# A fused attention and gated-unit kernel: the first batch's q loaded by GpSimd's casting DMA and transposed in bf16, k in five loads with the tail unit first, one DMA for the feature weights, and new order tables

## The chip, the cores and the metric

The kernel runs on one core of one Trainium2 chip. Its time is the device time in microseconds (us) of one execution; the runs of the kernel before took 214.36, 215.17 and 215.64 us, with a median of 215.17 us. The profile is of one further execution, whose time was 216.05 us; the span from its first to its last instruction is 214.3 us, so that 1.75 us lie around the span. A difference of about 0.5%, or 1.1 us, is the least that a measurement of this kernel can tell from no change.

## The reference

Eight batches of eight heads, 576 rows (`seq`) and 64 columns (`head_dim`). A linear attention with exponential features of both signs is followed by a gated unit with a causal filter of five taps:

```python
def phi(x):
    proj = np.einsum('bhsd,df->bhsf', x, w_phi)            # 64 -> 128 features
    proj = proj - np.max(np.abs(proj), axis=-1, keepdims=True)
    return np.concatenate([np.exp(proj), np.exp(-proj)], axis=-1)
q_p, k_p = (phi(q), phi(k))
kv = np.einsum('bhsf,bhsd->bhfd', k_p, v)
z = np.sum(k_p, axis=2)
num = np.einsum('bhsf,bhfd->bhsd', q_p, kv)
den = np.einsum('bhsf,bhf->bhs', q_p, z)[..., None] + 1e-06
x = num / den                                              # heads side by side: 512 columns
gate = 1.0 / (1.0 + np.exp(-gate_pre))                     # gate_pre: five taps of conv_w over x
out = gate * (x @ w_val) @ w_out
```

## The kernel before

**Tiling.** One batch holds 8 x 576 rows of q and as many of k. They are seen as 18 blocks of 128 columns, each block with two rows of 64 side by side, and the blocks are grouped into five units: `UNITS` has four units of four blocks and a tail unit of two (blocks 16 and 17). A batch passes through these stages: load of q, k and v; transposition of q and k (`qT`, `kT`); projection by the feature weights `W2` on TensorE (`kp` and `qm`, line 599); the maximum of the absolute value on VectorE (`kmax`, `qmax`, line 607); the exponentials on ScalarE (`kexp`, line 617, into the tile `KTIL`; `qexp`, line 732, into `QTIL`); the scaling of v on GpSimd (line 633); the products with the scaled v (line 643) and with q (line 744); the division (line 765); the gate (806), the value product (838) and the output product (860).

**What sets the order.** Nothing is scheduled when the kernel is built: the string `ORDER` gives the order in which the tasks of `build` are written out, `FLEX` gives the engine of each task that may run on several (A for ScalarE, D for VectorE, P for GpSimd), `BANKS` the PSUM banks, and `WARM` says ahead of which place in the order TensorE multiplies a tile of ones to no purpose (lines 514 and 517). Each engine takes its instructions strictly in that order, so an instruction that waits holds up all that stand behind it on its engine. The setup in `Emit.__init__` (constants, memsets, the weight load `c_w`) stands ahead of all tasks.

**The first batch.** Its k and q are loaded in fp32 by SyncE's queue into memory that the second batch's `KTIL` buffer needs later (`XN32`). k comes in four loads of 128x576, q in five, one to a unit, and after them comes the first batch's v (`loadv`, line 553). TensorE transposes each block in fp32 (`tp32`, line 558), and ScalarE or VectorE copies a unit out of PSUM with a cast to bf16 (`tc32`, lines 564 and 566). Two DMAs on ScalarE's queue load the same 64 rows of the feature weights into the two halves of `W32`; GpSimd casts them to `W2` (line 471), which every projection needs. A one-column copy named `hold` (line 531) makes GpSimd wait for q's last unit to land; behind it GpSimd's queue issues the casting loads of the second and third batch's q and k (line 572), of `w_val` (line 475) and of the second batch's v. The second batch is transposed in bf16 by TensorE (`tp16`, line 577) and copied out eight blocks at a time (`tc16`, line 582); from the third batch on DMA transposes do it (line 587). The loads by SyncE and ScalarE stand in the profile under "hardware_dynamic" queues (q1 and q10), those by GpSimd under "software_dynamic" (q0).

Of the kernel before, what the change touches and what calls it, by code (L numbers as in the profile page):

```python
# [16 lines left out]
B, H, S, D = 8, 8, 576, 64  # L17
# [7 lines left out]
NU = len(UNITS)  # L25
PEB = 1
# [10 lines left out]
    "16:7:1 16:7:1 16:7:0 16:7:0 16:7:0 16:7:0 16:7:0 16:7:0 16:7:0 16:7:0 16:7:0 16:7:0 16:7:0 16:7:0 16:7:0 16:7:0 "  # L37
    "16:7:0 16:7:0 "
# [43 lines left out]
)  # L82
FLEX = (
    "ADAADAAAAAPPDPPAPPPPPDDDDDDADDDDDDDPPDPPDPPPPPADDAAAAAPPDPPAPPPDPDDDDADDPPAPPAPPDPPDDDAADAAPPAPPAPPPPDDDAAAADPPAPPAPPP"
    "PDDDDADAAAPPDPPAPPPPPAADAAPDAPPDPPPPDADDDAA"
)
BANKS = (
    "0100170421234567014545456723670145320167456745014570123666230167676723676744233373266236723010101676701456767454545230"
    "1236767245013230123674545232301320532345450101670145452301674523014545016767001235446701456745672367246723670167454523"
    "0145672301012301452301452330167212672301234523452354235670123676767674545016723234501674501230146723444016745230145450"  # L90
    "1332401452301456767014567236745674501010123453672324423014545672345674253367010101010101452323672345676745670167010101"
    "45230145452367674554642323014523456767456723454501456701230145674522234545674567672355644"
# [21 lines left out]
def dve(n, ov=0.075):  # L114
    return n / 960.0 + ov
# [50 lines left out]
def build(plan, em=None):  # L166
# [16 lines left out]
    for b in range(B):  # L183

        if b == 0:
            last = A("lk", 0, 9, "SP", 0.3, None, rank=-1100)
            for w in "kq":
                lds = []
                for u in range(4 if w == "k" else NU):
                    pr = -1000.0 + (0 if w == "k" else 10) + u  # L190
                    last = A("l" + w, b, u, "SP", 0.65, fn("load32", w, u), [], rank=pr, lat=0.1)
                    lds.append(A("l" + w, b, u, "DMA", 0.9 if w == "k" else 0.2 * UNITS[u][1], None, [last], rank=pr))
                if w == "q":
                    hold = [None, A("lk", b, 0, "POOL", 0.15, fn("hold", HOLDU), [lds[HOLDU]], rank=-600)]
                for u, (c0, n) in enumerate(UNITS):
                    need = [lds[u]] if w == "q" else sorted(set(lds[J // 9] for J in (2 * c0, 2 * (c0 + n) - 1)), key=lambda t: t.idx)
                    pr = -900 + (0 if w == "k" else 50) + u
                    g = plan.group("tp", 1)
                    tp = A("kp", b, u, "PE", 0.22 * n, fn("tp32", w, u), need, g, 0, rank=pr)
                    h["x" + w, b, u] = A("kmax", b, u, ("DVE", "ACT"), (dve(n * P), act(n * P)), fn("tc32", w, u), [tp], g, rank=pr)  # L200
                    h["tp", w, u] = tp

        if b:
# [43 lines left out]
            for c in GB:  # L247
                if b == B - 1:
                    for x in h["gacc", c]:
                        x.deps += [x for x in (G("xk", b, 0), G("xq", b, 0)) if x is not None]  # L250
        if b == 1:
            g = plan.group("mqt", 1)
            cc = A("mqt", 0, 0, "PE", 0.5, fn("c_cw"), [G("tp", "q", 1)], g, rank=-500)
            cc = A("mqt", 0, 0, "DVE", 0.2, fn("c_cw2"), [cc], g, rank=-500)
            cgs = []
            for i in range(2):
# [689 lines left out]
```

## Time and profile before

| what | value |
|---|---|
| median of three runs | 215.17 us |
| time of the profiled execution | 216.05 us |
| its span | 214.3 us |
| busy: PE, ScalarE (ACT), VectorE (DVE), GpSimd (POOL) | 90%, 85%, 81%, 61% of the span |
| moved by DMA | 39.84 MB, 186 GB/s over the span |

A share of busy time over the whole span says little here, because the stages have other limits: at the start the engines wait for the first loads, in the middle three engines are nearly full at once, and at the end the last outputs are written. Rows of the timeline give the start in us, the length, the engine, the line, the operation and the tiles (written <- read); a name with a q behind the engine (SPq, ACTq) is an issue on that engine's queue. PEld is TensorE's loading of weights, which runs beside its products.

### The profile page before, as it was taken

What the parts mean: (1) busy time and instruction counts of PE and PEld (TensorE: products, weight loads), DVE (VectorE), ACT (ScalarE), POOL (GpSimd) and SP (SyncE); (2) the same over time, 40 slices, a digit from 0 to 9 for tenths busy, and PEclk for the clock granted to TensorE, in tenths of its full rate; (3) what the DMA queues carried; (4) which work ended last, traced back from release to release, by engine and by line L of the source; (5) the groups of instructions that cost most, each with busy time, mean ns of one, the idle gap of its engine ahead of it and who ended that gap; (6) DMA issues with size and microseconds to landing.
All of it is one profiled execution on the core that took longest, in us unless ns stands there. A gap on an engine that the chain in (4) does not pass through costs nothing.

```text
span 214.3 us, 8735 instructions
## 1 busy us (share of the span) xinstructions
PE 192.9 (90%) x3806; PEld 136.1 (64%) x3806; DVE 173.1 (81%) x258; ACT 181.1 (85%) x256; POOL 131.2 (61%) x167
## 2 busy tenths in 40 slices
PE   7995767898999999998999899999999999999990
PEld 6663455666665675766775667567776765888630
DVE  2679999989989988999988899989789978643630
ACT  3599999999999998999899998999999999544130
POOL 3577999992996199728990499459922578101100
PEclk9999999999999999999999999999999999999997
DMA  6999999569869968996999998999942606189095
GB/s 187 347 266 212 215 270 176 217 110 191 169 122 216 263 119 165 260 215 120 184 260 227 189 160 212 277 239 210 171 146 47 225 8 101 31 146 315 9 268 173
DMA packets 49425, 39.84 MB, mean 186 GB/s; under 512 B 33637, under 2 KB 39013, under 8 KB 49386
## 3 DMA queue, kind: packets, MB, share of 16 engines
q1 hardware_dynamic: 43088, 28.58, 56.6%
q0 software_dynamic: 6032, 10.49, 25.9%
q8 instruction: 30, 0.49, 0.9%
q10 hardware_dynamic: 266, 0.21, 0.3%
q14 instruction: 9, 0.07, 0.1%
HBM read 30.48 MB, written 9.44 MB: 186 GB/s over the span
## 4 chain that ended last, share of the span: by engine, by line
PE 48%; DVE 19%; ACT 17%; issue 7%; POOL 3%; DMA 2%; ACTq 0%; DVEq 0%; POOLq 0%
PE PS L860 10%; PE PS L838 10%; ACT KTIL L617 7%; PE PS L806 7%; DVE MQP L607 6%; ACT QTIL L732 5%; DVE MK L607 5%; PE PS L599 5%; PE PS L744 4%; PE PS L643 3%; DVE GV L844 2%; PE PS L719 2%; DMA W<-in_w_phi_dram 2%; DVE XN L765 2%; PE PS L864 2%
## 5 line engine op out<-in xcount | busy, mean ns | idle before, releaser
L617 ACT ACTIVATE KTIL<-PS 128x1024 bf16<-128x1024 f32 (+1 forms) x80 | 71.6, 966 | 3.0 <-PE PS L599 2.1
L633 POOL TENSOR_TENSOR VT<-VN,EK 128x1152 bf16<-128x1152 f32 x31 | 65.8, 2123 | 2.6 <-ACT EK L626 2.2
L732 ACT ACTIVATE QTIL<-PS 128x1024 bf16<-128x1024 f32 x64 | 61.7, 1049 | 1.9 <-PE PS L724 1.8
L705 POOL TENSOR_TENSOR RX<-MQR,ident 128x512 bf16<-128x512 bf16 (+1 forms) x35 | 34.3, 1008 | 36.6 <-DVE MQR L693 34.8
L607 DVE TENSOR_REDUCE MQP<-PS 128x8 bf16<-128x1024 f32 (+1 forms) x40 | 43.2, 1112 | 4.7 <-PE PS L599 3.2
L607 DVE TENSOR_REDUCE MK<-PS 128x8 f32<-128x1024 f32 (+1 forms) x40 | 44.1, 1112 | 3.5 <-ACT KTIL L617 2.3
L838 PE MATMUL PS<-XT,WV 128*128 128x288 bf16 x256 | 35.0, 286 | 0.3
L860 PE MATMUL PS<-WOUT,GV 128*128 128x512 bf16 x128 | 30.9, 379 | 0.1
L844 DVE SCALAR_TENSOR_TENSOR GV<-TH,PS 128x576 bf16<-128x576 bf16 x32 | 23.8, 749 | 7.7 <-PE PS L838 6.1
L838 PEld LDWEIGHTS <-WV 128*128 128x128 bf16 x256 | 23.8, 98 | 8.2 <-issue 1.9
L810 ACT ACTIVATE TH<-PS 128x576 bf16<-128x576 f32 x32 | 20.2, 675 | 5.6 <-DVE GV L844 3.1
L806 PE MATMUL PS<-XT,GW 64*64 64x288 bf16 x640 | 23.5, 285 | 0.4 <-DVE MK L607 0.2
L643 PE MATMUL PS<-VT,KTIL 64*128 64x65 bf16 x1152 | 22.6, 191 | 1.4 <-issue 0.6
L765 DVE TENSOR_TENSOR XN<-PS,RCP 128x512 bf16<-128x512 f32 x32 | 22.1, 692 | 1.1
L643 PEld LDWEIGHTS <-KTIL 64*128 64x128 bf16 x1152 | 20.7, 95 | 3.5 <-issue 2.1
L744 PEld LDWEIGHTS <-QTIL 128*128 128x128 bf16 x512 | 17.9, 97 | 7.1 <-issue 5.7
L657 ACT ACTIVATE OUTS<-PS 128x512 f32<-128x512 f32 x23 | 14.0, 617 | 9.9 <-PE PS L860 8.1
L744 PE MATMUL PS<-KV,QTIL 128*128 128x65 bf16 x512 | 19.7, 193 | 2.0 <-DVE KV L651 0.9
L806 PEld LDWEIGHTS <-GW 64*64 64x64 bf16 x640 | 18.0, 106 | 3.6 <-issue 1.9
L860 PEld LDWEIGHTS <-GV 128*128 128x128 bf16 x128 | 11.4, 98 | 12.7 <-issue 1.5
L599 PE MATMUL PS<-W,kT 64*128 64x128 bf16 x288 | 14.7, 221 | 3.3 <-ACT qT L566 1.3
L719 PE MATMUL PS<-qT,W 64*128 64x512 bf16 (+1 forms) x80 | 14.6, 361 | 3.0 <-DVE MQP L607 1.7
(80 smaller groups left out, 226.8 us busy)
## 6 DMA issues: line engine op xcount, KB each, us to landing
out_dram<-OUTS SPq DMA_DIRECT2D x32, 256.0 KB, 3.8
VN<-in_v_dram SPq DMA_DIRECT2D x7, 1152.0 KB, 6.2
KQN<-in_q_dram POOLq DMA_DIRECT2D x6, 576.0 KB, 6.6
KQN<-in_k_dram POOLq DMA_DIRECT2D x6, 576.0 KB, 10.0
KTIL<-in_k_dram SPq DMA_DIRECT2D x4, 288.0 KB, 3.8
VN<-in_v_dram POOLq DMA_DIRECT2D x1, 1152.0 KB, 19.0
KTIL<-in_q_dram SPq DMA_DIRECT2D x4, 256.0 KB, 4.5
out_dram<-OUTS SPq DMA_DIRECT2D x14, 64.0 KB, 2.6
```

Source lines behind the costliest of these rows:

```text
L607: self.nc.vector.tensor_reduce(o, self.two(t.grp, n * P).rearrange("p a (c f) -> p a c f", f=F), AX.X, ALU.max, apply_absolute_value=True)
L617: self.nc.scalar.activation(self.KTIL[b % 2][:, s, c0:c0 + n, :, :].rearrange("p c a f -> p a c f"), self.two(t.grp, n * P).rearrange("p a ...
L633: x.tensor_tensor(self.VT[g][:, s, :, 0:D], self.VN[b % 2][:, NC * g:NC * g + NC, :], e.to_broadcast([P, NC, D]), ALU.mult)
L643: nc.tensor.matmul(self.PS[:, t.grp.banks[ab], (s * 2 + x) * E1:(s * 2 + x + 1) * E1], self.KTIL[b % 2][rows, s, J // 2, J % 2, :], self.V ...
L705: self.nc.gpsimd.tensor_tensor(o, *wide(self.MQR[self.mq(b, u)][:, :], self.ident2), ALU.mult)
L732: self.nc.scalar.activation(o, i, AF.Exp, scale=1.0 - 2.0 * s)
L744: nc.tensor.matmul(self.PS[:, t.grp.banks[h // 4], (h % 4) * E1:(h % 4 + 1) * E1], Q[:, s, c % 2, h, (c // 2) * P:(c // 2 + 1) * P], self. ...
L765: nc.vector.tensor_tensor(o.rearrange("p (g h) d -> p g h d", g=ng), n[:, :, :, 0:D], rc.unsqueeze(3).to_broadcast([P, ng, 4, D]), ALU.mult)
L806: self.nc.tensor.matmul(self.PS[o * D:(o + 1) * D, t.grp.banks[par], 0:R], self.GW[r, jj, 4 - m, :], X[r, 4 * a + jj, :, HALO - 8 * s:HALO ...
L838: self.nc.tensor.matmul(self.PS[:, t.grp.banks[par], 0:R], self.WV[:, i, (2 * j + par) * D:(2 * j + par + 2) * D], X[:, 4 * par + i, :, HA ...
L844: nc.vector.scalar_tensor_tensor(out=self.GV[b % 3][:, j, :, :], in0=self.TH[j][:, :, :], scalar=1.0, in1=self.two(t.grp, R), op0=ALU.add, ...
L860: nc.tensor.matmul(self.PS[:, t.grp.banks[0], :], GV[:, j, c % 2, (c // 2) * XH:(c // 2) * XH + P], self.WOUT[:, j, c % 2, :], start=(j == ...
```

## The change

The first batch's q is no longer loaded in fp32 by SyncE. GpSimd issues two casting DMAs (`loadq0`) of blocks 8 to 17 and of blocks 0 to 7 into bf16, in that order, and TensorE transposes q in bf16 with `tp16`; ScalarE or VectorE copies out blocks 0 to 7, 8 to 15 and 16 to 17. `hold` now reads the last column of the load of blocks 8 to 17. k comes in five loads, the first of which (`KLOADS`) brings the columns of the tail unit alone (128x256) and the last the rest of that quarter (128x320). One DMA with a repeated source fills both halves of `W32`. The memset of `ONES` is cut in two, and all of the tables (`WARM`, `ORDER`, `FLEX`, `BANKS`) are new.

```diff
+KLOADS = [(3, 5, 9), (0, 0, 9), (1, 0, 9), (2, 0, 9), (3, 0, 5)]
...
-    "16:7:1 16:7:1 16:7:0 16:7:0 16:7:0 16:7:0 ...
+    "16:6:0 16:6:0 ... 16:6:1 16:6:1 16:0:2 18:1:3 71:6:2 203:3:1 80:6:2 76:1:2 "
...
-            for w in "kq":
-                lds = []
-                for u in range(4 if w == "k" else NU):
-                    last = A("l" + w, b, u, "SP", 0.65, fn("load32", w, u), [], rank=pr, lat=0.1)
+            for u in range(NU):
+                last = A("lk", b, u, "SP", 0.65, fn("load32", "k", u), [], rank=-1000.0 + u, lat=0.1)
...
+            for i in range(2):
+                last = A("lq", b, i, "POOL", 0.65, fn("loadq0", i), [], rank=-990.0 + i, lat=0.6)
+                lds.append(A("lq", b, i, "DMA", 2.2, None, [last], rank=-990.0 + i))
+            hold = [None, A("lk", b, 0, "POOL", 0.15, fn("hold"), [lds[1]], rank=-600)]
+            for i, (c0, n) in enumerate(((0, 8), (8, 8), (16, 2))):
+                tp = A("xq", b, i, "PE", 0.06 * n, fn("tp16", "q", b, c0, n), [lds[min(i, 1)]], g, 0, rank=-850 + i)
+                x = A("xq", b, i, ("DVE", "ACT"), (dve(n * P), act(n * P)), fn("tc16", "q", b, c0, n), [tp], g, rank=-850 + i)
...
-        nc.vector.memset(self.ONES[:, :], 1.0)
+        for c in ((0, P), (P, 512)):
+            nc.vector.memset(self.ONES[:, c[0]:c[1]], 1.0)
...
-        for i in range(2):
-            nc.scalar.dma_start(self.W32[i * D:(i + 1) * D, :], self.wphi[:, :])
+        nc.scalar.dma_start(self.W32[:, :], self.wphi[:, :].unsqueeze(0).to_broadcast([2, D, F]))
...
+    def loadq0(self, t, i):
+        sl = slice((0, 8)[i], (8, NC)[i])
+        self.nc.gpsimd.dma_start(self.N["q"][0][:, sl, :].rearrange("p y c -> p (y c)"), self.rows("q", 0)[:, sl.start * P:sl.stop * P])
```

The program's order shows the change at three places. The first is GpSimd's queue from the cast of the weights (`W`) to the loads of the second and third batch. Before:

```order
L458 MEMSET MQP_88 128x128
L471 CAST W_127<-W_126 128x128 [waits DMAHW2_49,DMAHW0_49]
L531 CAST HOLD<-KTIL_73 128x1 [waits DMAHW0_49]
L572 DMA QTIL_75<-in_q_dram 128x2304
L572 DMA QTIL_75<-in_k_dram 128x4x576
L572 DMA KQN_65<-in_q_dram 128x2304
L475 DMA WV<-in_moe_w_val_dram 128x4x512
```

and after the change:

```order
L468 MEMSET MQP_89 128x128
L480 CAST W_128<-W_127 128x128 [waits DMAHW0_49]
L543 DMA KTIL_73<-in_q_dram 128x1280
L543 DMA KTIL_73<-in_q_dram 128x1024
L539 COPY HOLD<-KTIL_73 128x1 [waits DMASW0_49]
L580 DMA QTIL_75<-in_q_dram 128x2304
L580 DMA QTIL_75<-in_k_dram 128x4x576
L484 DMA WV<-in_moe_w_val_dram 128x4x512
```

The first batch's two q loads (into the memory of `KTIL_73`) now stand behind the cast of the weights, and `hold` waits for the first of them. The second place is TensorE's queue in the first batch, after the weights' first use. Before, the second and third group of k's fp32 transposes (line 558) stand with projections (line 599) around them:

```order
L558 MATMUL PS<-ident_f,KTIL_73 128x128 [waits DMAHW3_49]
L558 MATMUL PS<-ident_f,KTIL_73 128x128 x3
L599 LDWEIGHTS kT_68 [waits Activation_49]
L599 MATMUL PS<-W_127,kT_68 128x128 [waits Pool_49]
...
L558 MATMUL PS<-ident_f,KTIL_73 128x128 [waits DMAHW5_49]
L558 MATMUL PS<-ident_f,KTIL_73 128x128 x3
L599 LDWEIGHTS kT_68 [waits DVE_49]
```

and after it, where line 566 is k's fp32 transpose, line 585 q's bf16 transpose and line 607 the projection:

```order
L566 MATMUL PS<-ident_f,KTIL_73 128x128 [waits DMAHW3_49]
L566 MATMUL PS<-ident_f,KTIL_73 128x128 x3
L585 LDWEIGHTS KTIL_73 [waits DMASW0_49]
L585 MATMUL PS<-ident,KTIL_73 128x128
...
L566 MATMUL PS<-ident_f,KTIL_73 128x128 [waits DMAHW4_49,Activation_49]
L566 MATMUL PS<-ident_f,KTIL_73 128x128 x3
L607 LDWEIGHTS kT_68
L607 MATMUL PS<-W_128,kT_68 128x128 [waits DVE_49]
```

Eight transposes of q, which wait for the first of GpSimd's loads (DMASW0), now stand between k's transposes of unit 0 and the first projection of that unit. The third place is the head of ScalarE's queue. Before:

```order
L472 DMA cw_141<-in_moe_conv_w_dram 5x512
L566 ACT_TABLE_LOAD
L566 CAST kT_68<-PS 128x512 [waits PE_49]
L617 ACTIVATE KTIL_72<-PS 128x2x4x128 [waits PE_49]
L566 CAST qT_70<-PS 128x512 [waits PE_49]
```

and after the change:

```order
L481 DMA cw_142<-in_moe_conv_w_dram 5x512
L625 ACT_TABLE_LOAD [waits DVE_49]
L625 ACTIVATE KTIL_72<-PS 128x2x2x128 [waits PE_49]
L625 ACTIVATE KTIL_72<-PS 128x2x2x128
L574 CAST kT_68<-PS 128x512 [waits PE_49]
```

The table load now stands behind a wait for VectorE's copy of the tail unit, and the tail unit's two exponentials come first. SyncE's queue holds the five k loads and then the first batch's v, none of which waits for anything. Over the whole program ScalarE gets 5 of the copies named `KV` where it had 10, 21 of the output copies where it had 23, and one large and one small copy of `XT` less; VectorE takes these over; the one scaling of v that VectorE did (and its small cast) goes to GpSimd.

More of the change, by code (lines that the diff above doesn't have):

```diff
@@ L36 @@
 WARM = (
-    "16:7:1 16:7:1 16:7:0 16:7:0 16:7:0 16:7:0 16:7:0 16:7:0 16:7:0 16:7:0 16:7:0 16:7:0 16:7:0 16:7:0 16:7:0 16:7:0 "
-    "16:7:0 16:7:0 "
+    "16:6:0 16:6:0 16:6:0 16:6:0 16:6:0 16:6:0 16:6:0 16:6:0 16:6:0 16:6:0 16:6:0 16:6:0 16:6:0 16:6:0 16:6:0 16:6:0 "
+    "16:6:1 16:6:1 16:0:2 18:1:3 71:6:2 203:3:1 80:6:2 76:1:2 "
 )
@@ L44 @@
 ORDER = (
[37 rows of a table removed]
[36 rows of a table added]
 )
 FLEX = (
-    "ADAADAAAAAPPDPPAPPPPPDDDDDDADDDDDDDPPDPPDPPPPPADDAAAAAPPDPPAPPPDPDDDDADDPPAPPAPPDPPDDDAADAAPPAPPAPPPPDDDAAAADPPAPPAPPP"
-    "PDDDDADAAAPPDPPAPPPPPAADAAPDAPPDPPPPDADDDAA"
+    "ADAADADAPPDPPDPPPPPDDDADDADDDDDDAPPDPPDPPPPPDDDAADAAPPDPPDPPDPPDDDDAAAPPAPPAPPPPPDDAAADADPPDPPAPPPPPDDDADADPPDPPAPPPPD"
+    "DDDADDDAPPAPPDPPPPPDADADPPDPPDPPDPPAADAAD"
 )
 BANKS = (
[L88 to L92, printed above, removed]
+    "2245023301674523012367012345236702014545672323452232344523012323450123674365363617345012301452323670167016745670101456"
+    "7674542301574670145670145014523207674567450123234523676701672301454523672346767522016767454567230161620123676701230101"
+    "6723230123234501454545230456743501232323232323673127367010123670167454545676745230101230101232672330767012367010123231"
+    "2046745674523452301454567234501674545450145545674260123456701230123225320101450145230167676723016767232345670101676734"
+    "676701450167454504516767454545670145236767670123454501670145016733234501010123452310550"
 )
@@ L186, in build @@
             last = A("lk", 0, 9, "SP", 0.3, None, rank=-1100)
-            for w in "kq":
-                lds = []
-                for u in range(4 if w == "k" else NU):
-                    pr = -1000.0 + (0 if w == "k" else 10) + u
-                    last = A("l" + w, b, u, "SP", 0.65, fn("load32", w, u), [], rank=pr, lat=0.1)
[L192 to L201, printed above, removed]
+            lds = []
@@ new lines, in build @@
+            for u in range(NU):
+                last = A("lk", b, u, "SP", 0.65, fn("load32", "k", u), [], rank=-1000.0 + u, lat=0.1)
+                lds.append(A("lk", b, u, "DMA", 0.9, None, [last], rank=-1000.0 + u))
+            for u, (c0, n) in enumerate(UNITS):
+                need = sorted(set(lds[i] for i, (hp, a, z) in enumerate(KLOADS) for J in (2 * c0, 2 * (c0 + n) - 1) if a <= J - 9 * hp < z), key=lambda t: t.idx)
+                g = plan.group("tp", 1)
+                tp = A("kp", b, u, "PE", 0.22 * n, fn("tp32", "k", u), need, g, 0, rank=-900 + u)
+                h["xk", b, u] = A("kmax", b, u, ("DVE", "ACT"), (dve(n * P), act(n * P)), fn("tc32", "k", u), [tp], g, rank=-900 + u)
+                h.setdefault(("tp0",), []).append(tp)
@@ new lines, in build @@
+            lds = []
+            for i in range(2):
[3 more added lines that the diff above has]
+            for i, (c0, n) in enumerate(((0, 8), (8, 8), (16, 2))):
+                g = plan.group("tp", 1)
+                tp = A("xq", b, i, "PE", 0.06 * n, fn("tp16", "q", b, c0, n), [lds[min(i, 1)]], g, 0, rank=-850 + i)
+                x = A("xq", b, i, ("DVE", "ACT"), (dve(n * P), act(n * P)), fn("tc16", "q", b, c0, n), [tp], g, rank=-850 + i)
+                h.setdefault(("tp0",), []).append(tp)
+                for u, (d0, m) in enumerate(UNITS):
+                    if c0 <= d0 < c0 + n:
+                        h["xq", b, u] = x
@@ L273, in build @@
                                        [kp] + [G("st", b - 2, i, x) for i in range(2) for x in range(2)]
-                                       + ([G("tp", w, i) for i in range(NU) for w in "kq"] if b == 1 else []), g)
+                                       + (G("tp0",) if b == 1 else []), g)
         eks = []
@@ L405, in __init__ @@
         spare = self.KTIL[1][:, :, :, :, :].rearrange("p s c a f -> p s (c a f)").bitcast(FP32)
-        self.XN32 = {w: spare[:, i, :] for i, w in enumerate("kq")}
+        self.XN32 = {"k": spare[:, 0, :]}
+        self.N["q"][0] = self.KTIL[1][:, 1, :, :, :].rearrange("p c a f -> p (c a f)")[:, 0:NR].rearrange("p (y c) -> p y c", c=2 * D)
         spare = self.QTIL[1][:, :, :, :, :].rearrange("p s a h r -> p (s a h r)")
@@ L527, in zero, with hold @@
                                       start=False, stop=True, skip_group_check=True)
-    def hold(self, t, u):
-        c = UNITS[u][0] * P
-        self.nc.gpsimd.tensor_copy(self.HOLD[:, :], self.XN32["q"][:, c:c + 1])
+    def hold(self, t):
+        self.nc.gpsimd.tensor_copy(self.HOLD[:, :], self.N["q"][0][:, NC - 1, 2 * D - 1:2 * D])
+    def loadq0(self, t, i):
+        sl = slice((0, 8)[i], (8, NC)[i])
+        self.nc.gpsimd.dma_start(self.N["q"][0][:, sl, :].rearrange("p y c -> p (y c)"), self.rows("q", 0)[:, sl.start * P:sl.stop * P])
     def holdx(self, t, b):
@@ L543, in load32 @@
         o = self.XN32[w]
-        if w == "q":
-            c0, n = UNITS[u]
-            sl = slice(c0 * P, (c0 + n) * P)
-            self.nc.sync.dma_start(o[:, sl], self.rows("q", 0)[:, sl])
-        else:
-            self.nc.sync.dma_start(o[:, u * 9 * D:(u + 1) * 9 * D], self.rows("k", 0)[:, u, :])
+        hp, a, z = KLOADS[u]
+        self.nc.sync.dma_start(o[:, (hp * 9 + a) * D:(hp * 9 + z) * D], self.rows("k", 0)[:, hp, a * D:z * D])
     def loadv(self, t, b):
```

2 lines of the change are left out of this document (1 added, 1 removed), and 73 rows, old and new, of the table ORDER.

## The prediction

> **What bounds the kernel now.** I read the slices of the page first, then a table of five stretches, then the timeline of the first 16 us.
>
> ```profile
> span 214.3 us, 8735 instructions
> PE   7995767898999999998999899999999999999990
> DVE  2679999989989988999988899989789978643630
> ACT  3599999999999998999899998999999999544130
> ```
>
> Each digit is the busy tenth of 5.4 us. After the first three or four slices ACT and DVE are full, and PE is full from about the ninth on; no engine bounds the whole.
>
> ```profile
> core 0: us, PE busy (x) PEld busy (x) DVE busy (x) ACT busy (x) POOL busy (x), PEclk, DMA share, GB/s
> 0.00:11.60 11.60, 9.76 (x68) 7.56 (x68) 4.94 (x10) 5.55 (x7) 5.82 (x19) 1.00 0.83 273
> 11.60:40.00 28.40, 20.34 (x442) 14.82 (x437) 26.98 (x40) 28.08 (x43) 25.38 (x25) 1.00 1.13 234
> 40.00:180.00 140.00, 134.61 (x2837) 94.19 (x2835) 125.82 (x184) 134.37 (x188) 97.06 (x119) 1.00 0.84 176
> 180.00:207.00 27.00, 26.61 (x462) 19.04 (x460) 14.63 (x25) 12.13 (x20) 2.96 (x7) 1.00 0.57 147
> ```
>
> From 11.6 to 40 us ACT works 28.08 of 28.4 us and DVE 26.98, while PE idles 8.06 us waiting for them. From 40 to 180 us PE and ACT have 5.4 and 5.6 us of idle time left, and in the next 27 us PE has 0.4. So a microsecond lost ahead of 11.6 us, where ACT works only 5.55 of 11.6 us, is carried to the end, but for what these few idle microseconds give back. The prediction is decided at the start.
>
> ```profile
> 0.74 1.22 ACTq L470 DMA_DIRECT2D W<-in_w_phi_dram  x2
> 2.77 1.28 ACT L566 ACT_TABLE_LOAD   x1 [2.77 <-issue]
> 5.76 0.29 POOL L471 CAST W<-W 128x128 bf16<-128x128 f32 x1 [3.21 <-DMA W<-in_w_phi_dram]
> 6.75 1.02 ACT L617 ACTIVATE KTIL<-PS 128x1024 bf16<-128x1024 f32 x1 [1.14 <-PE PS L599]
> 10.51 0.59 ACT L566 CAST qT<-PS 128x512 bf16<-128x512 f32 x1 [1.15 <-PE PS L558]
> 20.36 5.66 ACT L732 ACTIVATE QTIL<-PS 128x1024 bf16<-128x1024 f32 x6
> ```
>
> The weights' cast waits until 5.76 us for the second weight DMA, the first large exponential starts at 6.75, ACT is full from 10.51, and q's first exponential starts at 20.36. Six of those take 5.66 us, so one costs ACT 0.94 us in a row (they overlap a little).
>
> **The change part by part: when q lands.** This term decides. The new loads of q stand behind the weights' cast on POOL, and PE stands still at the first of q's transposes, since all of its other work is queued behind. What the trace says of GpSimd's loads:
>
> ```profile
> 43.42 0.59 POOL L572 DMA_DIRECT2D KQN<-in_q_dram  x1
> q0 software_dynamic: 10, 0.05, 112.6%
> ```
>
> The issue at 43.42 us met idle DMA engines, and its first packets show in the window from 44.5 to 45 (the row; the half microsecond ahead of it has none), so first packets come about 1.3 us after the issue began. With SyncE's queue busy it is otherwise:
>
> ```profile
> 8.13 0.73 POOL L572 DMA_DIRECT2D QTIL<-in_q_dram  x1
> q1 hardware_dynamic: 298, 0.68, 99.7%
> q0 software_dynamic: 13, 0.06, 30.0%
> q0 software_dynamic: 44, 0.20, 99.4%
> ...
> 68.98 0.61 POOL L572 DMA_DIRECT2D KQN<-in_q_dram  x1 [0.32 <-issue]
> q1 hardware_dynamic: 268, 0.61, 103.3%
> q0 software_dynamic: 18, 0.08, 97.6%
> ```
>
> Behind the issue at 8.13 stand the queues from 10 to 12 us (q1, SyncE's, alone), 12 to 13 and 13 to 14; behind that at 68.98 the windows 69.5 to 71 (q1 alone) and 71 to 71.5. Both times GpSimd's packets came only as SyncE's v load ran out, 4 and 2 us after the issue. Once they flow they bring 0.20 MB (of bf16) per us.
>
> ```profile
> KTIL<-in_k_dram SPq DMA_DIRECT2D x4, 288.0 KB, 3.8
> VN<-in_v_dram SPq DMA_DIRECT2D x7, 1152.0 KB, 6.2
> QTIL<-in_q_dram POOLq DMA_DIRECT2D x1, 576.0 KB, 8.5
> q1 hardware_dynamic: 274, 0.56, 79.6%
> q1 hardware_dynamic: 220, 0.37, 101.6%
> ```
>
> After the change SyncE's queue holds k (4 x 288 KB) and right behind it v (1152 KB), issued without a wait in six issues of some 0.44 us, so by 3.4 us; before, v was issued at 6.49 us, behind q. These are 2.36 MB. The queue brought 0.56 MB from 2 to 4 us and 0.37 MB from 7 to 8 (the last two rows). At 0.36 MB per us from 4 us on, k ends at (1.18 - 0.6) / 0.36 = 1.6, so 5.6 us, with the weights' packets 5.8, and v at 5.8 + 1.18 / 0.36 = 9.0 us.
>
> ```profile
> DMA to landing us min/median/max: 3.3/3.8/4.3
> ```
>
> Of the two weight DMAs (this row, and the issue at 0.74 above) one landed 3.3 and one 4.3 us after its issue. The single one should land between 4.0 and 5.0 us; I take 4.4. The cast starts 0.14 us behind the landing as before (5.62 to 5.76) and takes 0.29, so q is issued at 4.85 us and is ready to flow at 6.15: just after v has begun at 5.8. I take it that q waits for v, as in both cases above: packets from 9.0 us, 0.33 MB (128 x 1280 x 2 bytes) at 0.20 gives 10.65, and from the last packet to the landing 1.0 us, as for QTIL (0.59 MB from about 12.7 end at 15.65, landed at 8.13 + 8.5 = 16.63). **q's first load lands at 11.6 us**, the second at 12.9. The ends: 8.8 (q goes ahead of v: 6.15 + 1.65 + 1.0) and 12.5 (a weight DMA that is a microsecond slower, and slower first packets).
>
> [...]
>
> **What follows from the landing.**
>
> ```profile
> L558 PE MATMUL PS<-ident_f,KTIL 128*128 128x128 f32 x36 | 8.5, 391 | 0.1
> L577 PE MATMUL PS<-ident,QTIL 128*128 128x128 bf16 x36 | 2.7, 220 | 0.0
> 7.68 0.61 PE L599 MATMUL PS<-W,kT 64*128 64x128 bf16 x8
> 13.80 0.40 PE L599 MATMUL PS<-W,kT 64*128 64x128 bf16 x8
> ```
>
> After 11.6 us PE does eight bf16 transposes (8 x 2.7 / 36 = 0.6), four fp32 ones (4 x 8.5 / 36 = 0.95) and a unit's eight projections at the early rate (0.61), so unit 0's exponential starts at about 13.8 us. The rest of ACT's queue up to q's first exponential is eight large exponentials (8 x 0.94 = 7.5), a copy of 1024 columns (1.0), two of 256 (0.6), two casts of 512 (1.0) and two small exponentials (0.35): 10.45 us, so 24.3 us where before it was 20.36. Two more small exponentials follow it that came ahead of it before. **ACT is 4.2 us late there.** PE gives the same: before, its useful work by 11.6 us was 9.76 less 2.5 for the products of ones, so 7.3 us; after the change it has done 0.5 + 0.3 + 0.95, so 1.75, and saves 18 x (8.5 - 2.7) / 36 = 2.9 us in all. 7.3 - 1.75 - 2.9 is 2.65, with 1.1 us for the three products of ones that come later 3.8 us. I take 4.0.
>
> The table load, hidden at 2.77 before, now starts behind the tail unit's copy, at some 5 us; its 1.28 us and the tail's two exponentials end by 7.5 us and lie inside the wait for q. Without that wait the table load would cost up to 1.3 us. The k order, the split memset and the longer run of products of ones cost nothing for the same cover. VectorE's copy of q (0.69) and its next cast end at 13.95, beside PE's work. The second batch's loads begin behind `hold` at 11.8 instead of 8.13, but flow from 13.1 where before from 12.7: 0.4 us, and they are wanted from 18 us before, 22 after; nothing.
>
> **What is given back.**
>
> ```profile
> L657 ACT ACTIVATE OUTS<-PS 128x512 f32<-128x512 f32 x23 | 14.0, 617 | 9.9 <-PE PS L860 8.1
> L655 ACT CAST KV<-PS 128x520 bf16<-128x520 f32 x10 | 6.2, 615 | 1.2 <-PE PS L643 0.5 <-PE PS L685 0.4
> L655 ACT COPY XT<-PS 128x1024 bf16<-128x1024 bf16 x1 | 1.1, 1081 | 0.0
> ```
>
> The new tables take five KV copies, two output copies, a large and a small XT copy off ACT behind the start: 5 x 0.62 + 2 x 0.62 + 1.08 + 0.37 = 5.8 us, and lay most of it on DVE. That is worth something only where ACT ends last; PE, with 5.4 us idle in 140, cannot regain more than that, and DVE, 95% busy from 11.6 to 40 us, gets more work. Bounds: 4.0 given back in full and 1.8 more (ACT alone the bound), or nothing and 0.5 lost. By the nearest row, PE's, I take 1.0. The sum is 4.0 - 1.0 = 3.0 us later: 219.0 us against the profiled execution's 216.05, and against the median of 215.17, 0.9 us lower, **218.2 us**.
>
> **The rivals.**
> - *q slips in ahead of v.* If the weights land at 4.0 us, q is ready at 5.75, about as k ends. Landing at 8.8 instead of 11.6 takes 2.8 us off: 218.2 - 2.8 is 215.4. For it speaks how near the two times are; against it, both issues above. [...]
> - *The new tables win behind the start (the other side).* ACT was full from 11.6 to 40 us and 96% busy to 180; if it and not PE decides, all of its 5.8 us counts against 4.0: 213.4. It decides from the point where more than 4.0 us is given back. Against it: PE's 0.4 us of idle time in 180 to 207, and that the work goes to DVE.
> - *The hole costs more.* PE's projections went from 0.61 to 0.40 us per unit only after some 12 us of steady work; a stand of five microseconds puts that off for about five units, 1.0 us, and if weights and q land at the late end (0.9) and nothing is given back: 218.2 + 1.0 + 0.9 + 0.4, so 220.5.
> - *The change doesn't do what it says:* excluded by the order, which shows each part.
>
> **How the numbers follow.** The forecast has 0.52 (its own range 216.4 to 220.0), q ahead of v 0.17, the tables 0.17, the larger hole 0.14. About 0.5% or 1.1 us is the least that a measurement of this kernel tells from no change, so the middle reaches from 214.1 to 216.3. Faster: the tables and 0.01 of the second case, 0.18. Same: most of the second case and the forecast's low edge, 0.18. Slower: 0.64. The range from 214.6 to 221.0 leaves out the tables' case and a little above.
>
> **What would show it.** In the changed profile PE should idle from about 6 us to 11.6, ended by the DMA of q, with q0's first packets near 9 us; the first 1024-wide exponential should start near 13.8 and q's first near 24.3. Packets of q0 by 6.5 us, or a first large exponential ahead of 11, would make it wrong at the first step; a late start with a span of 214 or less, at the give-back.

## The result and the profile after

The changed kernel takes 223.63 us (median; 222.89 to 225.99), the kernel before 215.4 us on the same chip. The ratio is 1.0395 with a 95% interval of 1.034 to 1.0451: slower, and above the forecast's range. The profiled execution took 222.89 us, the lowest of its runs, with a span of 221.1 us against 214.3. The medians of the kernel before differ by up to 3 us from chip to chip, so kernels are compared below by their ratios to the kernel before on the same chip. Ratios leave out the slower executions (over 1.5% above the fastest of their kernel) and medians don't; the profiles of v_behind_q, fast_front, fast_front_old_back, k_first and k_first_old_back are of such slower executions.

The page's slices, a fortieth of the span (5.5 us) to a digit:

```profile
span 221.1 us, 8726 instructions
PE   6177766798999999799999998999999899999980
ACT  1339999999998999899999997999999879344230
```

The four stretches that were shown of before (the last is longer here, to 214 us, and is not compared):

```profile
core 0: us, PE busy (x) PEld busy (x) DVE busy (x) ACT busy (x) POOL busy (x), PEclk, DMA share, GB/s
0.00:11.60 11.60, 4.68 (x31) 3.36 (x31) 2.95 (x8) 2.85 (x4) 3.29 (x15) 0.88 0.85 250
11.60:40.00 28.40, 20.70 (x400) 14.51 (x401) 25.86 (x33) 25.13 (x35) 23.71 (x26) 0.93 1.01 190
40.00:180.00 140.00, 132.15 (x2808) 92.22 (x2804) 125.92 (x187) 132.00 (x183) 98.47 (x118) 1.00 0.85 179
180.00:214.00 34.00, 33.88 (x581) 22.93 (x580) 20.26 (x38) 14.97 (x23) 8.10 (x16) 1.00 0.62 129
```

PE works 4.68 of the first 11.6 us where it worked 9.76, and from 40 to 180 us it idles 7.85 us (140 less 132.15) where it idled 5.4. The second loss was not in the forecast, which had PE regain a little there. The start, in rows of the timeline:

```profile
0.73 1.18 ACTq L479 DMA_DIRECT2D W<-in_w_phi_dram  x1
4.77 1.28 ACT L625 ACT_TABLE_LOAD   x1 [4.77 <-DVE kT L572]
6.22 0.29 POOL L480 CAST W<-W 128x128 bf16<-128x128 f32 x1 [3.83 <-DMA W<-in_w_phi_dram]
6.46 1.27 POOL L543 DMA_DIRECT2D KTIL<-in_q_dram  x2
12.40 1.03 PE L585 MATMUL PS<-ident,KTIL 128*128 128x128 bf16 x8 [4.95 <-DMA KTIL<-in_q_dram]
14.87 1.02 ACT L625 ACTIVATE KTIL<-PS 128x1024 bf16<-128x1024 f32 x1 [6.41 <-PE PS L607]
24.88 1.02 ACT L740 ACTIVATE QTIL<-PS 128x1024 bf16<-128x1024 f32 x1
```

The weights' cast starts at 6.22 us, q is issued at 6.46 and has landed at 12.40 us; PE stands 4.95 us for it. The queues (q1 is SyncE's, with v; q0 GpSimd's, with q) from 8 to 9, 9 to 10 and 11 to 12 us:

```profile
q1 hardware_dynamic: 170, 0.38, 96.7%
q0 software_dynamic: 7, 0.02, 10.7%
q0 software_dynamic: 53, 0.14, 72.7%
q1 hardware_dynamic: 73, 0.15, 38.4%
q1 hardware_dynamic: 13, 0.02, 6.1%
q0 software_dynamic: 99, 0.19, 100.0%
```

Issued at 6.46 us, q's packets come as v runs out, near 9 us, and from 11 us on at 0.19 MB per us, as forecast.

### The profile page after: what moved, and what is told of

Same layout as the page of the kernel before. It is cut to its first block, busy times and chain, and to the rows that moved or that the text cites. A ratio compares the mean times of both kernels' runs of the same rounds, so it can differ in the third digit from the quotient of the medians.

```text
span 221.1 us, 8726 instructions
## 1 busy us (share of the span) xinstructions
PE 192.2 (87%) x3813; PEld 133.2 (60%) x3813; DVE 175.0 (79%) x264; ACT 176.1 (80%) x245; POOL 133.6 (60%) x173
## 4 chain that ended last, share of the span: by engine, by line
PE 50%; DVE 23%; DMA 13%; POOL 5%; issue 4%; ACT 3%; DVEq 0%
PE PS L846 11%; DVE MQP L615 10%; PE PS L868 9%; PE PS L814 8%; DMA kT<-KQN 6%; PE PS L607 5%; DVE MK L615 5%; PE PS L651 4%; PE PS L752 3%; DMA KTIL<-in_q_dram 3%; PE PS L727 3%; POOL VT L641 3%; DMA W<-in_w_phi_dram 2%; DVE XN L773 2%; DMA XT<-XN 2%
## 5 line engine op out<-in xcount | busy, mean ns | idle before, releaser
L641 POOL TENSOR_TENSOR VT<-VN,EK 128x1152 bf16<-128x1152 f32 x32 | 68.0, 2124 | 14.5 <-DMA VN<-in_v_dram 11.3
L868 PE MATMUL PS<-WOUT,GV 128*128 128x512 bf16 x128 | 31.4, 379 | 0.2 <-ACT KV L663 0.2
L651 PE MATMUL PS<-VT,KTIL 64*128 64x65 bf16 x1152 | 23.1, 191 | 1.8 <-POOL VT L642 0.6
L665 ACT ACTIVATE OUTS<-PS 128x512 f32<-128x512 f32 x21 | 12.4, 609 | 10.9 <-PE PS L868 10.3
L607 PE MATMUL PS<-W,qT 64*128 64x128 bf16 x288 | 14.8, 220 | 2.8 <-DVE MQP L615 1.2
```

The costliest lines, as they stand in the source:

```text
L607: nc.tensor.matmul(self.PS[:, t.grp.banks[par], i * P:(i + 1) * P], X[rows, (c0 + i) * P:(c0 + i + 1) * P], self.W2[rows, :], start=True, ...
L641: x.tensor_tensor(self.VT[g][:, s, :, 0:D], self.VN[b % 2][:, NC * g:NC * g + NC, :], e.to_broadcast([P, NC, D]), ALU.mult)
L651: nc.tensor.matmul(self.PS[:, t.grp.banks[ab], (s * 2 + x) * E1:(s * 2 + x + 1) * E1], self.KTIL[b % 2][rows, s, J // 2, J % 2, :], self.V ...
L868: nc.tensor.matmul(self.PS[:, t.grp.banks[0], :], GV[:, j, c % 2, (c // 2) * XH:(c // 2) * XH + P], self.WOUT[:, j, c % 2, :], start=(j == ...
```

## The experiments

Theory: the start's lag makes the loss, carried to the end. Rivals: the new tables cost something themselves; the idle stretch costs through TensorE's clock (`PEclk`, the share of full speed that it was granted).

### Mending one part of the start

Four kernels, each the changed kernel with one edit.

```diff
 q_first: GpSimd issues both loads of q, then waits for the weights
-        self.nc.gpsimd.tensor_copy(self.W2[:, :], self.W32[:, :])      (in c_w)
+        if i == 0:                                                    (in loadq0, behind its DMA)
+            self.nc.gpsimd.tensor_copy(self.W2[:, :], self.W32[:, :])
 v_behind_q: GpSimd issues v behind q; SyncE's loadv(0) does nothing
+            self.nc.gpsimd.dma_start(self.VN[0]..., self.rows("v", 0))  (in loadq0)
 two_w: the weights by two DMAs
-        nc.scalar.dma_start(self.W32[:, :], self.wphi[:, :].unsqueeze(0).to_broadcast([2, D, F]))
+        for i in range(2):
+            nc.scalar.dma_start(self.W32[i * D:(i + 1) * D, :], self.wphi[:, :])
 warm_hole: twelve products of ones ahead of q's first transposes
-80:6:2 76:1:2 "
+80:6:2 76:1:2 25:1:24 "
```

> The changed kernel with the weights' cast moved behind the two q loads in GpSimd's queue, so that q is issued at about 2.4 us instead of 6.46. In the changed kernel q landed at 12.38 us and the first exponential of 1024 columns began at 14.87. Theory 1 (q waits for the weights' cast, then for the first batch's v on SyncE's queue, and the tables only carry this lag on): q's packets start by 4 us between the k loads, q lands at 6.5 to 7.5, the first large exponential begins at 9 to 10, and the lag against before at q's first exponential, 4.5 us in the changed kernel, vanishes; the time falls by 5 us or more, to 215 to 218.5. Theory 2 (the new tables behind the start are themselves slower, as the lag grows from 4.5 us at 25 us to 7.2 us at the end): the start improves as much, but 2 to 3 us over before stay, 217.5 to 218.5. Theory 3 (GpSimd's packets yield to SyncE's queue as long as it has any): q's packets still start at 8.5 to 9 us, q lands near 12 and the time stays at 223.

> The changed kernel with the first batch's v issued by GpSimd behind the two q loads instead of by SyncE behind k; q's issue stays at 6.46 us behind the weights' cast. If q's first packets (at about 9 us in the changed kernel) waited for v, they now start 1.3 us after the issue, at 7.8; q lands at 10.4 instead of 12.38, and the time falls by about 2 us, to 221.5. If GpSimd's loads need that long by themselves, q lands at 12.4 and the time stays at 223.5.

> The changed kernel with the two weight DMAs of before instead of the one with a repeated source. The single one landed at 6.17 us, 5.4 us after its issue. If the repeated source is what made it slow (few DMA engines, as its packets came at 40 per us from 3 to 6 us), the pair lands at 5.0 to 5.6 as before, q is issued some 0.6 us earlier; q lands at 11.8 to 12.4 and the time falls by 0 to 0.6 us, since v on SyncE's queue still stands ahead of q. If the weights are slow for another reason, the weights land near 6.2 again and nothing changes.

> The changed kernel with twelve products of ones (512 columns each, into an unused bank) ahead of q's first transposes on TensorE, where it stands idle from 7.5 to 12.4 us. If the dip of the granted clock (0.88 up to 11.6 us, 0.76 from 11.6 to 20) costs what it takes off PE there, about 1 us, the dip goes and the time falls by about 1 us, to 222.5. If ACT and DVE set the pace in that stretch all the same, the clock is back at 1.00 and the time stays within 0.5 us.

| kernel | weights' cast | q landed | first large exponential | ratio (95%) |
|---|---|---|---|---|
| changed | 6.22 | 12.40 | 14.87 | 1.0395 (1.034 to 1.0451) |
| q_first | 6.30 | 10.00 | 12.47 | 1.0382 (1.0316 to 1.0448) |
| v_behind_q | 5.70 | 10.41 | 12.88 | 1.0265 (1.017 to 1.0361) |
| two_w | 5.10 | 13.13 | 15.60 | 1.0471 (1.0361 to 1.0581) |
| warm_hole | 6.28 | 12.49 | 14.39 | 1.0334 (1.0259 to 1.0409) |

With v out of the way, q issued at 5.94 us lands 4.5 us later, at 10.41; with v ahead it took 5.9 us (6.46 to 12.40). So about 1.5 us of the wait were v's, and the other 0.5 us came from the earlier issue. With two weight DMAs the cast starts 1.1 us earlier, yet q does not land earlier: v stands ahead of it either way. q_first issues q at 2.33 us, ahead of v, and it lands only at 10.00, where 6.5 to 7.5 was expected: q and v then share the DMA engines, as the queues from 6 to 7 us show.

```profile
q0 software_dynamic: 52, 0.13, 71.6%
q1 hardware_dynamic: 63, 0.10, 30.5%
```

Still q is 2.4 us earlier, and the time is not: the changed kernel's projections that start at 38.79 us start at 36.39 in q_first, but those that start at 45.79 start at 45.96. warm_hole shortens the stretch at half clock in the hole from 6.83 to 3.4 us and starts the first large exponential 0.5 us earlier; its ratio is 0.6% lower. The intervals overlap, as do those of v_behind_q and two_w with the changed kernel's, so what the clock in the hole costs is within the noise here (0.6% is some 1.3 us). Either a lead is not carried whole behind the new tables, or something else takes it. A second set of experiments therefore takes start and tables apart.

### Start and tables crossed

These kernels take the loads and the first 90 emitted steps of `ORDER`, with their engines and banks, from one kernel, and all steps behind from the other kernel's tables. The edit is in the tables alone, here that of new_front_old_back against the changed kernel (its order leaves out steps that emit nothing):

```diff
 FLEX = (
-    "ADAADADAPPDPPDPPPPPDDDADDADDDDDDAPPDPPDPPPPPDDDAADAAPPDPPDPP...
+    "ADAADADAPPDPPAPPPPPDDDDDDADDDDDDAPPDPPDPPPPPADDAAAAAPPDPPAPP...
```

fast_front is the changed kernel with q_first, v_behind_q and two_w together and four products of ones (`25:1:8`); fast_front_old_back has the old tables behind it.

> The first 90 steps and the loads are those of the kernel before (q by SyncE in float32, k in four loads, two weight DMAs, the old order), all behind them follows the new tables (order, engines, banks). Theory 'the start alone': the first large exponential stands near 6.8 us and q's first near 20.4 as before, and the time is that of before, 214.5 to 216.5. Rival 'the new tables are slower behind the start too' (the lag of the changed kernel grew from 4.5 us at q's first exponential to about 6.8 at the end): 217 to 218.5. Rival 'the new tables win behind the start' (the forecast's give-back): 213 or less.

> The first 90 steps, the loads and the weights are those of the changed kernel, all behind them follows the old tables. The start alone: q's first exponential near 24.9 as in the changed kernel, the time that of the changed kernel, 222 to 224. The new tables are slower: 219.5 to 221 (before and the lag of 4.5, with up to 1 us more). The new tables win: over 224.

> The changed kernel with its hole mended: GpSimd issues both loads of q and then v, and only then waits for the weights' cast; two weight DMAs; four products of ones ahead of q's first transposes. The tables are the new ones. All theories: q lands at 7.5 to 9, the first large exponential at 9.5 to 11, q's first at 21 to 22.5, so 2.5 to 4 us earlier than in the changed kernel. The start alone: 218 to 220.5 (the whole lead is carried to the end). The new tables are slower: the same, but 1.5 to 2.5 us above its lag at q's first exponential. A third, that the lead is lost in a stall of TensorE near 42 us, as in q_first: 220.5 to 223.

> The mended start of fast_front with the old tables behind the first 90 steps. The start alone: within 1 us of fast_front. The new tables are slower: 1.5 to 2.5 us below fast_front, 216 to 218. If TensorE's stall near 42 us comes from the order of the new tables there (v's load ahead of q's transposing DMA), it is gone here.

> The changed kernel once more, on the same chip as the next one: 222.5 to 225.

> The changed kernel's first 90 steps with the old tables behind, on the same chip as the changed kernel. If the start is the whole loss: within 0.6 us of the changed kernel. If the new tables cost 1 to 2.5 us beside it behind this start (the traces have 218.9 and 221.1 us of span): 1 to 2.5 us below it. If their order is worth something behind this start, as the forecast's give-back had it: 0.6 us or more above it.

| kernel | q's first exponential | median | ratio (95%) |
|---|---|---|---|
| old_front_new_back | 19.04 | 221.02 | 1.0281 (1.0185 to 1.0378) |
| new_front_old_back | 25.17 | 221.7 | 1.0334 (1.0244 to 1.0423) |
| fast_front | 21.78 | 222.79 | 1.0274 (1.0148 to 1.0401) |
| fast_front_old_back | 22.19 | 218.97 | 1.0193 (1.0103 to 1.0282) |
| after_again | 25.17 | 226.98 | 1.0436 (1.037 to 1.0502) |
| new_front_old_back_again | 25.94 | 221.59 | 1.0187 (1.0142 to 1.0232) |

The last two ran on the same chip, where the kernel before took 217.25 us: the changed start with the old tables is 4.3 us slower than before, and the new tables behind the same start cost another 5.4 us. The sizes are not that firm. In their first measurements, each set beside its own runs of the kernel before, the same two kernels differ by 0.6% only (1.0395 against 1.0334, some 1.3 us), and fast_front and fast_front_old_back differ by 0.8%; in both pairs the intervals overlap. So by these pairs the start costs some 4 to 7 us and the new tables some 1 to 5.4; the sign is the same each time. That "the start is the whole loss" falls, by the pair on one chip, and that the new tables win behind it is seen nowhere. How exactly the old tables carry the start shows in rows of the timeline: q's first exponential (of before shown in the forecast, 20.36 us), the first value product behind the last numerator, and the last products. Of before, and then of new_front_old_back_again:

```profile
187.31 1.14 PE L838 MATMUL PS<-XT,WV 128*128 128x288 bf16 x8
207.52 1.05 PE L864 MATMUL PS<-WOUT,GVT 128*64 128x512 bf16 x8
```

```profile
25.94 1.02 ACT L737 ACTIVATE QTIL<-PS 128x1024 bf16<-128x1024 f32 x1
192.96 1.14 PE L843 MATMUL PS<-XT,WV 128*128 128x288 bf16 x8
213.17 1.05 PE L869 MATMUL PS<-WOUT,GVT 128*64 128x512 bf16 x8
```

With before's 20.36 us the lags are 5.58, 5.65 and 5.65 us: in this run nothing is given back in 187 us. The times follow the lags less closely: fast_front_old_back, with q's first exponential 1.83 us late, is 1.9% (some 4 us) slower than before. The new tables seem to have a price behind an early start too: old_front_new_back is 1.0281, though its first q exponential starts earlier than before's. But any of these splices may have a price of its own at the seam, and no run prices it.

### Where in the new tables

Two loads were moved in the order, two splices set elsewhere, and k was put ahead of q at the start.

```diff
 after_v, fast_front_v, old_front_v (SyncE's steps; the same move in the changed kernel,
 in fast_front and in old_front_new_back)
 xpose q 6
+loadv 6
 odma x5, xpose k 7, odma, xpose q 7
-loadv 6
 after_qt
 xpose k 2
-loadv 2
 xpose q 2
+loadv 2
 old_tail: the changed kernel, steps from 870 on by the old tables
 late_seam: the kernel before, steps from 170 on by the new tables
 k_first: fast_front, k's units 0 to 3 ahead of q in the first 90 steps, q's first eight blocks loaded first,
 without products of ones behind the weights; k_first_old_back: old tables behind it
```

> The kernel before up to its first numerator product (170 steps, 38 us), all behind follows the new tables. If the new tables lose in the stretch from 20 to 40 us only (old_front_new_back stood 1.2 us late there): 214.5 to 216.5, as before. If they lose behind 40 us too (TensorE idles 5.7 us from 40 to 100 us in the changed kernel, 3.7 before) or in the tail: 217 to 220.

> The changed kernel; only the last 100 or so steps (from the last batch's q exponentials on, some 35 us) follow the old tables. If the new tables' tail costs the 1.0 us of TensorE and 0.6 us of last output DMA that the trace shows behind the last numerator: 1.0 to 1.7 us below the changed kernel, ratio 1.031 to 1.035. If TensorE's backlog decides and the tail only passes it on: within 0.6 us of the changed kernel.

> fast_front with another order in the first 90 steps: TensorE and ScalarE take k's units 0 to 3 ahead of q's transposes, so that nothing stands behind q's landing (near 9.6 us); of q the first eight blocks are loaded first; no products of ones behind the weights. The tables behind the first 90 steps are the new ones. If the hole comes from q's place in TensorE's queue: the first large exponential at 6.5 to 8 us (changed kernel 14.9), q's first exponential at 18 to 20.5 (24.9). The start alone: 215 to 217.5, since a start as early as that of before is carried to the end. The new tables are slower: 217 to 220. If q's landing itself were needed that early: first large exponential early, but q's first exponential not before 22, and 218 or more.

> k_first with the old tables behind the first 90 steps. The start alone: within 1 us of k_first. The new tables are slower: 213.5 to 216, 1.5 to 4 us below k_first.

> The changed kernel; only v's load of the seventh batch is issued by SyncE right behind that batch's transposing DMA of q (near 131 us) instead of behind the eighth batch's two transposing DMAs (155 us). GpSimd's wait of 10.7 us for it near 152 us goes. If the late v is a bound of the new tables that already costs the changed kernel its growth of lag: 220 to 221.5. If TensorE's backlog from the start covers it there (TensorE is busy 30.0 of the 30 us from 140 to 170 us): the time of the changed kernel, 222.5 to 224.

> fast_front with the same move of v's load. If the late v is the second bound, on which an earlier start runs up: 1.5 to 3 us below fast_front, near 219 (as fast_front_old_back). If the new tables are slower elsewhere: as fast_front, 221.5 to 223.

> old_front_new_back (start of the kernel before, new tables behind) with the same move of v's load. If the late v is what the new tables cost with an early start: 216 to 218.5, against 221.0 (ratio 1.028) with the late load. If not: 220.5 to 222.

> The changed kernel; only v's load of the third batch goes behind that batch's transposing DMA of q on SyncE, as in the kernel before (in the changed kernel the transposes stand behind it and their issue takes 6.3 us near 37 us instead of 3.6). If this is where TensorE's extra 1 to 2 us of idle time between 40 and 100 us come from: 221 to 222.5. If that load is off the path: as the changed kernel, 222.5 to 224.

| kernel | ratio (95%) | without the edit |
|---|---|---|
| late_seam | 1.0322 (1.0254 to 1.039) | 1 |
| old_tail | 1.0476 (1.041 to 1.0542) | 1.0395, 1.0436 |
| k_first | 1.0445 (1.0382 to 1.0508) | 1.0274 |
| k_first_old_back | 1.031 (1.0249 to 1.037) | 1.0193 |
| after_v | 1.0668 (1.0598 to 1.0739) | 1.0395, 1.0436 |
| fast_front_v | 1.049 (1.043 to 1.055) | 1.0274 |
| old_front_v | 1.0474 (1.04 to 1.0547) | 1.0281 |
| after_qt | 1.0443 (1.0375 to 1.051) | 1.0395, 1.0436 |

late_seam is slower, with the kernel before left as it is for 38 us, but its seam holds part of that: PE stands 2.06 us there and then has its clock halved from 38.65 to 45.48 us (PEclk 0.50 from 40 to 44 us), so it does not price the tables. old_tail found nothing: the products left behind the last numerator are not the loss, or its seam costs as much. k_first has its first large exponential at 7.39 us, as expected, but q's first only at 25.40, the outcome that was to speak for q's landing. q had landed by 11.61 us, though; in its order the units wait for VectorE's copies and maxima (PE up to 1.33 us at a time), and PE ran at half its clock from 9.2 to 26.2 us (PEclk 0.79 over the first 40 us). It was no mended start, and doesn't settle what q's landing is worth. Its pair is the second in which the new tables are slower clear of the intervals: 1.0445 against 1.031, some 2.9 us.

The late v was the best suspect. GpSimd waits 10.66 us for it in the changed kernel, and not at all by the old tables:

```profile
151.62 3.49 SPq L595 DMA_TRANSPOSE qT<-KQN  x1
155.17 0.58 SPq L561 DMA_DIRECT2D VN<-in_v_dram  x1
162.40 2.12 POOL L641 TENSOR_TENSOR VT<-VN,EK 128x1152 bf16<-128x1152 f32 x1 [10.66 <-DMA VN<-in_v_dram]
```

Issued at 134.21 us instead it made all three kernels some 2 to 2.7% slower, outside every expectation. SyncE's queue of after_v, and the waits of ACT and PE from 128 to 156 us (us in total, times, longest):

```profile
134.21 0.54 SPq L558 DMA_DIRECT2D VN<-in_v_dram  x1
134.80 2.02 SPq L882 DMA_DIRECT2D out_dram<-OUTS  x3
```

```profile
ACT OUTS L662 <- DMA out_dram<-OUTS: 4.6, 1, 4.6
PE PS L604 <- ACT OUTS L662: 3.9, 2, 3.6
```

The load now stands ahead of the outputs; ACT waits 4.6 us for an output's DMA to land before it writes the next one, and PE 3.6 us for ACT; PE's clock is then halved from 143.83 to 150.65 us (PEclk 0.88 from 125 to 150 us). So the move trades GpSimd's wait for a dearer one, and the late place is what lets the outputs pass in this order. In the changed kernel PE works 29.99 of the 30 us from 140 to 170, so GpSimd's wait was covered there; the late v is not shown to be the tables' price.

The profiles show one stall that comes and goes. after_again, the changed kernel a second time (span 225.4 against 221.1 us):

```profile
42.39 0.41 PE L759 MATMUL PS<-KV,QTT 128*64 128x65 bf16 x14 [0.19 <-DVE XN L773]
44.65 0.24 PE L759 MATMUL PS<-KV,QTT 128*64 128x65 bf16 x2 [1.85 <-issue]
```

In the middle of a run of 16 PE stands 1.85 us for nothing that the profile names, and then works at half its clock for 3.41 us (PEclk 0.50). What this and the other stretches cost is seen beside new_front_old_back_again, whose rows are the second fence (0 to 40, 40 to 60, 60 to 150 and 150 to 185 us):

```profile
0.00:40.00 40.00, 25.34 (x425) 18.13 (x426) 28.62 (x41) 27.76 (x39) 26.82 (x41) 0.87 0.92 207
40.00:60.00 20.00, 15.43 (x326) 11.08 (x324) 15.14 (x23) 16.24 (x23) 13.09 (x16) 0.91 0.80 137
60.00:150.00 90.00, 87.47 (x1896) 60.73 (x1894) 83.37 (x126) 85.95 (x119) 64.99 (x81) 1.00 0.89 188
150.00:185.00 35.00, 32.95 (x616) 22.44 (x612) 30.33 (x43) 30.08 (x43) 21.76 (x24) 1.00 0.63 157
```

```profile
0.00:40.00 40.00, 24.45 (x412) 17.66 (x413) 26.90 (x39) 26.78 (x38) 25.90 (x40) 0.87 0.90 202
40.00:60.00 20.00, 16.74 (x430) 12.84 (x430) 18.84 (x30) 20.00 (x28) 16.23 (x20) 1.00 0.82 155
60.00:150.00 90.00, 86.68 (x1810) 60.08 (x1808) 81.49 (x122) 85.99 (x121) 63.58 (x78) 1.00 0.96 201
150.00:185.00 35.00, 34.62 (x692) 24.34 (x691) 30.43 (x47) 33.67 (x49) 23.11 (x27) 1.00 0.57 129
```

From 40 to 60 us, behind the stall, PE does 326 products where the old tables let it do 430, and ACT is busy 3.8 us less. From 60 to 150 us the new tables catch up: up to there PE has done 2647 products in the one and 2652 in the other. From 150 to 185 us they are 76 products behind again and PE idles 1.7 us more, 1.2 us of it in one wait for GpSimd's scaled v. Counted in products, then, the loss that stays arises behind 150 us (products differ in length, so this is a rough count). The first profile of the changed kernel, which has no stall, falls behind in neither stretch (424 products from 40 to 60 us, 707 from 150 to 185).

The stall stands in five profiles (q_first 1.93 us, v_behind_q 2.57, two_w 1.31, fast_front 2.14, after_again 1.85), all of kernels in which the new tables issue the third batch's v ahead of its transposing DMA of q, and in none with the old tables behind; but other kernels with that order, the changed kernel's first profile among them, have none. after_qt, which turns these two round, has none in its profile, but is not faster. So the stall stands where q_first loses its lead, but is not shown to be the tables' price. Which part of the new order costs the 1 to 5.4 us stays open; no kernel here beats the kernel before.

## Why the prediction was right and wrong

- **The start decides and is carried: right for the start, but it does not decide alone.** The forecast had a lag of 4.0 us; in the changed kernel q's first exponential was 4.5 us late. The old tables behind the changed start show 4.3 us of time (221.59 against 217.25) and 5.65 us in the trace of a run that began later; the first measurement of the same kernel has 3.3% or some 7 us.
- **The weights land at 4.0 to 5.0 us: wrong.** They landed at 6.17 us, and the cast began at 6.22. The weights were 1.8 us later than the 4.4 us taken, q 0.8 us, since it waited for v in any case. In the profiles with two weight DMAs the cast started at 4.62 to 5.94 us (5.10 in two_w), in those with one at 5.70 to 6.30, so the repeated source is later by some 0.9 us on average, though not in every pair. Why it is later, no run shows.
- **q waits for v: right.** 11.6 us was forecast, 12.40 measured; without v ahead 10.41, where the working of the lower end gives 5.94 + 1.3 + 1.65 + 1.0 = 9.9. It holds for a q issued behind v: issued ahead of it, in q_first, q shared the engines with v and took 7.7 us.
- **The table load is hidden: right** (4.77 us, inside the wait).
- **First large exponential 13.8, q's first 24.3:** 14.87 and 24.88. PE's eight transposes took 1.03 us, not 0.6: it was at half its clock (PEclk 0.50 from 8.74 to 15.57 us).
- **The give-back of 1.0 us: wrong in its sign, and the step that failed.** It was bounded by the work moved off ACT (at best 5.8 us, at worst 0.5 us lost), and the 1.0 between was a choice without a sum. In the changed kernel's first profile the lag grew from 4.5 us at q's first exponential to 6.8 us at the end of the span, in the second from 4.8 to 11.1: 2.3 and 6.3 us were lost behind the start. The pairs with the same start put the loss at some 1 to 5.4 us, and none shows a gain. ACT did get 5.0 us less to do (181.1 to 176.1 us busy), near the 5.8 forecast, and it bought nothing. That the same work waits for other work at other places is the likely reason, but which waits these are stays open. The lower bound should have been open.
- **The rivals.** q did not slip ahead of v. The tables did not win. The larger hole (220.5 us) came nearest to the time, but not by its mechanism: its extra microseconds were to come from the start, and in both profiles most came from behind it. Its sum was also off: with nothing given back it should have added the whole 1.0 us, not 0.4, which gives 221.1. That the new tables lose more than 0.5 us was no rival at all.

So the direction came from the start, whose lag at q's first exponential was sized well, and most of what is missing from 218.2 to 223.63 us from a term that was given the wrong sign.

## What to carry to other kernels

When a change brings a regenerated order, treat the order as a change of its own: splicing one kernel's start to the other's rest tells whether both cost something, which totals by engine cannot; for the sizes, run each pair on one chip, more than once. A lag at the start can be carried whole where the engines behind it idle only a few microseconds, as in the trace above (5.58 us at the start, 5.65 at the end). And a load moved ahead of outputs on one queue can cost more than the wait that it removes (about 2% here), because the outputs hold the tiles that the next copies need (in after_v ACT waited 4.6 us for one).

## What the runs showed of the hardware

The granted clock of TensorE differs between executions of one kernel: its mean over the span is 0.960 to 0.991 in the six of after_again. In the changed kernel's first profile it is halved for 6.83 us from 8.74 us on, in and behind the hole:

```profile
8.74:15.57 6.83, 3.17 (x32) 2.46 (x34) 1.59 (x3) 0.70 (x1) 3.17 (x6) 0.50 0.80 157
44.72:48.13 3.41, 3.41 (x39) 2.46 (x40) 2.21 (x6) 1.30 (x4) 1.02 (x2) 0.50 0.40 90
```

The second row is of after_again, behind the stall; the first stretch is twice as long as the second (6.83 against 3.41 us). In the 3.41 us ahead of the second row TensorE worked 1.14 us, in the 3.42 us ahead of the first 0.88, both at a PEclk of 1.00:

```profile
41.31:44.72 3.41, 1.14 (x32) 1.00 (x31) 1.89 (x5) 3.41 (x4) 3.41 (x3) 1.00 1.19 154
5.32:8.74 3.42, 0.88 (x8) 0.53 (x7) 0.69 (x1) 2.30 (x4) 1.50 (x3) 1.00 0.99 344
```

So both times TensorE had been idle for some two thirds or more of that stretch (67% and 74%), and in warm_hole, with products of ones in the hole, the stretch at half clock is 3.4 us instead of 6.83. What halves the clock, and how much of the scatter between executions comes from it, is not shown.

The column can also say 1.00 where the rows say otherwise: in new_front_old_back it reads 1.00 from 12 to 16 us,

```profile
12.00:16.00 4.00, 3.32 (x36) 2.60 (x38) 1.74 (x3) 0.85 (x1) 3.31 (x6) 1.00 0.54 82
```

and its timeline has

```profile
14.50 0.61 PE L604 MATMUL PS<-W,kT 64*128 64x128 bf16 x8
18.33 0.40 PE L604 MATMUL PS<-W,qT 64*128 64x128 bf16 x8 [0.52 <-ACT qT L589]
```

Eight projections take 0.61 us there and 0.40 later. In the changed kernel the same eight take 0.61 us at 14.22 us, where its column says 0.50, so by its durations TensorE was at the lower clock in new_front_old_back too. The durations, not the column, told the clock at this program's start.
